# Sliding-window attention into a gated feed-forward: the first v loads, the GpSimd queue and the planned arrival times

## The chip, the core and the metric

The kernel runs on one core of a Trainium2 chip. The metric is the device time of one execution in microseconds (us). "Before" was run nine times; its median is 320.32 us, the fastest run 319.82 and the slowest 321.81. Engines are named PE (matrix products), DVE (VectorE), ACT (ScalarE), POOL (GpSimd) and SP (SyncE). Loads are issued from POOL's instruction queue, in order with POOL's other work, and are carried out by 16 shared DMA engines.

## The reference

Eight batches, eight heads, 576 positions, head width 64. Heads 0 to 3 attend to the last 32 positions ("plain"); heads 4 to 7 attend to 32 positions at a stride of 4 ("dilated"). The result, 4608 rows of 512, goes through two matrix products with a gate between them.

```python
mask_plain = (rel >= 0) & (rel < window)                       # window = 32
mask_dil = (rel >= 0) & (rel < window * dilation) & (rel % dilation == 0)   # dilation = 4
scores = scale * np.matmul(q, k.transpose(0, 1, 3, 2))         # masked, softmax over the last axis
x = (attn @ v).transpose(0, 2, 1, 3).reshape(B * S, H * D)
h = x @ w_in                                                   # 512 -> 2048
g = h * (1.0 / (1.0 + np.exp(-h)))
out = g @ w_out                                                # 2048 -> 512
```

Inputs and output are float32; inside, the kernel works in float16 with float32 sums. The cast of q, k, v and the weights is done by the loads themselves, which POOL issues.

## The kernel before

**Tiles.** Attention runs per batch. For batches 0 to 2 k and q are loaded as rows (`nat`) and turned on PE (steps TD, TA, TR, TS, TB); later batches are turned by DMA. Scores (steps S) are computed in sets, exponentiated on ACT into `probs`, and multiplied with v (steps P for plain heads with tile `vp`, steps D for dilated heads with tile `vd`). DVE divides by the row sums (L659, L660). Steps XP and XD turn the result into x. Layer 1 (L861) makes 16 blocks h per group of rows, ACT makes tanh (L870), DVE makes gT (L872), and layer 2 (L894) needs all 16. The first two groups have 256 rows, the others 512.

**v of the first batch.** `vraw` holds v for the dilated heads in two halves. A copy brings each half into `vd`, whose last column of ones gives the row sums: half 0 by step V 0, on DVE (L481), and half 1 by the entry `c0` of the load list, on POOL (L232). Tile `vp` is filled by two loads, the first of only 96 rows (L178, below 32 rows of zeros written by L183), the second of the other 23 windows (L179).

**Masks.** For the first batch the mask is added to the scores on PE (L595). It comes from a tile `band`, which POOL makes (L194, L196) and DVE turns into `mask_d` and `mask_p` (L202 to L206).

**The order of loads** is written out by hand and issued by POOL after the first loads:

```python
ORDER = "k0 r0 w0a w0b c0 w1 w2 w3 d1 p1 r1 o0 v1 o1 o2 o3".split()
```

Here k0 are the last 48 rows of k and q, r0 is the second half of `vraw`, w0a to w3 are w_in in column blocks of 256 or 512, d1, p1, r1 and v1 are k and q (dilated, then plain), `vraw` and `vp` of batch 1, and o0 to o3 are w_out in four parts.

**The planner.** The order of PE, ACT and DVE instructions is found by a small model at build time (class `Plan`). It gives each step a cost and each load an arrival time: `AT_DIL`, `AT_PLAIN`, `AT_VRAW`, `AT_VP` for the first tiles of a batch, and for the list a running sum that starts at `AT_W0` and grows by `LOAD_US` for each entry. A step is placed no earlier than the arrival that it needs. On the chip nothing waits for a planned time: the times decide only the order in which each engine's instructions stand. `best` chooses between DVE and ACT for copies.

Of the kernel before, what the change touches and what calls it, by code (L numbers as in the profile page):

```python
# [10 lines left out]
F32 = mybir.dt.float32  # L11
# [5 lines left out]
def kernel(  # L17
# [9 lines left out]
    nc = tc.nc  # L27
    B, H, S, D = q.shape
    DM, DFF = moe_w_in.shape
    P = 128  # L30
    W = 32
# [5 lines left out]
    QB = P - W  # L37
# [14 lines left out]
    XR = 3  # L52
    NA = GA * GT
    BIG = 32768.0
    ORDER = "k0 r0 w0a w0b c0 w1 w2 w3 d1 p1 r1 o0 v1 o1 o2 o3".split()
    LOAD_US = {"w": 2.75, "o": 2.6, "d": 3.7, "p": 3.7, "r": 1.4, "v": 2.6, "k0": 2.0, "r0": 1.2, "c0": 0.0, "w0a": 1.4, "w0b": 1.4}
    AT_W0 = 10.6
    BIASED = (0,)

    cpool = ctx.enter_context(tc.tile_pool(name="const", bufs=1))  # L60
# [14 lines left out]
    xRs = [cpool.tile([P, HP, GT], F16, name=f"xR_{i}") for i in range(XR)]  # L75
# [4 lines left out]
    vps = [cpool.tile([P, HN * NB, 66], F16, name=f"vp_{i}") for i in range(NV)]  # L80
    vds = [cpool.tile([P, 2, HN, DIL, 66], F16, name=f"vd_{i}") for i in range(NV)]
    vraws = [cpool.tile([P, 2, HN, DIL, D], F16, name=f"vraw_{i}") for i in range(NV)]
# [23 lines left out]
    def nat_of(b, key):  # L106
        i = ("k", "q", "rest").index(key)
        return nats[b % 2][:MA, i * RW : (i + 1) * RW].rearrange("p (h r d) -> p h r d", h=H, r=DIL)
# [5 lines left out]
    def issue_nat(b, h0, h1):  # L114
        for nm, src, m0 in (("k", k, 0), ("q", q, MR)):
            rows = src[b].rearrange("h (m r) d -> m h (r d)", r=DIL)
            r0 = M - MR if nm == "k" else 0
            p0 = 0 if nm == "k" else MR
            for d, at in ((nat_of(b, nm), m0), (nat_of(b, "rest")[p0 : p0 + MR], r0)):
                nc.gpsimd.dma_start(  # L120
                    out=d[:, h0:h1].rearrange("p h r d -> p h (r d)"),
                    in_=rows[at : at + d.shape[0], h0:h1],
                )

    def issue_part(src, m0, m1, dst, h0, h1):
        rows = src[0].rearrange("h (m r) d -> m h (r d)", r=DIL)
        nc.gpsimd.dma_start(  # L127
            out=dst[: m1 - m0, h0:h1].rearrange("p h r d -> p h (r d)"), in_=rows[m0:m1, h0:h1]
        )

    def issue_first(h0, h1):
        issue_part(k, 0, MA, nat_of(0, "k"), h0, h1)
        issue_part(q, 0, MA, nat_of(0, "q"), h0, h1)
# [22 lines left out]
    def issue_vraw(b, halves=(0, 1)):  # L156
        vraw = vraws[b % NV]
        src = v[b, HN:].rearrange("h (m r) d -> m h (r d)", r=DIL)
        for ab in halves:
            p0, m0, m1 = ((0, 0, VA), (VB - KB, VB, M))[ab]  # L160
            nc.gpsimd.dma_start(  # L161
                out=vraw[p0 : p0 + m1 - m0, ab].rearrange("p h r d -> p h (r d)"),
                in_=src[m0:m1],
            )

    def v_win(t0, n, step=S * D):
        flat = v.rearrange("b h s d -> (b h s) d")
        win = flat[t0 : t0 + P]
        return bass.AP(
            tensor=win.tensor, offset=win.offset, ap=[win.ap[0], [step, n], win.ap[1]]  # L170
        )

    def issue_vp(b):
        nc.gpsimd.dma_start(out=vps[b % NV][:, :, :D], in_=v_win(b * H * S - W, HN * NB, QB * D))  # L174

    def issue_vp_first():
        flat = v.rearrange("b h s d -> (b h s) d")
        nc.gpsimd.dma_start(out=vps[0][W:, 0, :D], in_=flat[:QB])  # L178
        nc.gpsimd.dma_start(out=vps[0][:, 1:, :D], in_=v_win(QB - W, HN * NB - 1, QB * D))  # L179

    for t in vraws[::-1]:
        nc.vector.memset(t, 0.0)
    nc.vector.memset(vps[0][:W, 0, :], 0.0)  # L183
    nc.vector.memset(kqDs[0][:, :, :, 0, MA:], 0.0)
    for t in vps:
        nc.vector.memset(t[:, :, D:], 1.0)
# [1 line left out]
        nc.vector.memset(t[:, :, :, :, D:], 1.0)  # L188
    for t in kPs:
        nc.vector.memset(t[:, :, :W], 0.0)  # L190
    issue_first(HN, H)
    issue_first(0, HN)
    make_identity(nc, ident)
    nc.gpsimd.memset(band, 1.0)  # L194
    for s, base in ((1, 0), (-1, W - 1)):
        nc.gpsimd.affine_select(  # L196
            out=band, in_=band, compare_op=ALU.is_ge, fill=0.0, base=base,
            pattern=[[s, P]], channel_multiplier=-s,
        )
    issue_vraw(0, (0,))  # L200
    issue_vp_first()
    nc.vector.tensor_scalar(band, band, 1.0, BIG, ALU.subtract, ALU.mult)  # L202
    nc.vector.tensor_copy(mask_d[:, :6], band[:, None, :MH].broadcast_to([P, 6, MH]))
    nc.vector.tensor_copy(mask_d[:, 6:], band[:, None, P - MH :].broadcast_to([P, 4, MH]))
# [9 lines left out]
    AT, AT_WIN = {}, {}  # L214
    at = AT_W0
    for what in ORDER:
        kind, n = what[0], int(what[1])
        if kind == "w":
            f0, f1 = {"": (0, 4), "a": (0, 2), "b": (2, 4)}[what[2:]]
            cols = slice((4 * n + f0) * P, (4 * n + f1) * P)  # L220
            nc.gpsimd.dma_start(out=w_in16[:, :, cols], in_=wi[:, :, cols])  # L221
        elif kind == "o":
            nc.gpsimd.dma_start(
                out=w_out16[:, 4 * n : 4 * n + 4], in_=wo[:, 4 * n : 4 * n + 4]
            )
        elif what == "k0":
            issue_part(k, MA, M, nat_of(0, "rest"), 0, H)
            issue_part(q, MA, M, nat_of(0, "rest")[MR:], 0, H)
        elif what == "r0":
            issue_vraw(0, (1,))  # L230
        elif what == "c0":
            nc.gpsimd.tensor_copy(vds[0][:, 1, :, :, :D], vraws[0][:, 1])  # L232
        elif kind == "d":
            issue_nat(n, HN, H)
        elif kind == "p":
            issue_nat(n, 0, HN)
        elif kind == "r":
            issue_vraw(n)
        else:
            issue_vp(n)  # L240
        at += LOAD_US[what] if what in LOAD_US else LOAD_US[kind]
        AT[what] = at
        if kind == "w":
            for f in range(f0, f1):
                AT_WIN[4 * n + f] = at
# [83 lines left out]

    plan = Plan()  # L330
    t2 = at
    AT_DIL = {0: 5.4, 1: AT["d1"], 2: t2 + 7.0}
    AT_PLAIN = {0: 7.5, 1: AT["p1"], 2: t2 + 7.0}
    AT_VRAW = {0: 8.6, 1: AT["r1"], 2: t2 + 8.6}
    AT_VP = {0: 10.6, 1: AT["v1"], 2: t2 + 11.4}
    AT_CAST = t2 + 18.0
    AT_REST = AT["k0"]
    AT_V1 = AT["r0"] + 1.2
    AT_WOUT = [AT[f"o{n}"] for n in range(4)]

    readers = {}
# [94 lines left out]
    def attention(b):  # L436
        pe_path = b < PEB
        at_vraw, at_vp = (AT_VRAW[b], AT_VP[b]) if b < 3 else (v_in[b], v_in[b])
        sets, masks, home = SETS[pe_path], MASKS[pe_path], HOME[pe_path]
# [37 lines left out]
        def copy_on(eng, dst, src):  # L477
            if eng == "ACT":
                nc.scalar.copy(dst, src)  # L479
            else:  # L480
                nc.vector.tensor_copy(dst, src)  # L481

        def best(dve, act):
            ends = {
                e: max(plan.now, plan.free[e]) + us for e, us in (("DVE", dve), ("ACT", act))
            }
            return ("DVE", dve) if ends["DVE"] + LEAN * (b == 0) <= ends["ACT"] else ("ACT", act)
# [139 lines left out]
        def paired(key):  # L627
            step = best(0.335, 0.95)
            yield step
            src = nat_of(b, key)  # L630
            copy_on(
                step[0], pairs[key].rearrange("p g r i d -> p i g r d"),
                src[:, :HP].rearrange("p (g i) r d -> p i g r d", i=2),
            )
# [4 lines left out]
                nc.vector.tensor_scalar(t, t, 1.0 / BIG, 1.0, ALU.mult, ALU.add)  # L639

        def vd_of(ab):
            if b == 0 and ab == 1:
                return
            step = best(0.335, 0.95) if pe_path else ("DVE", 0.335)
            yield step
            copy_on(step[0], vd[:, ab, :, :, :D], vraws[b % NV][:, ab])
# [107 lines left out]
        for key in order:  # L754
# [3 lines left out]
            if kind == "N":  # L758
                st = Step(lambda ring, a=a: paired(*a), 0.0, (), [AT_PLAIN[b]], ("DVE",))
            elif kind == "B":  # L760
# [3 lines left out]
            elif kind == "TA" and b == 0:  # L764
                st = Step(
                    lambda ring, a=a: trans_a0(ring, *a), 0.36, rings,
                    [AT_PLAIN[0]],
                )
            elif kind == "TD" and b == 0:
                st = Step(lambda ring, a=a: trans_d0(ring, *a), 0.17, rings, [AT_DIL[b]])  # L770
            elif kind == "TR":
# [12 lines left out]
            elif kind == "TD":  # L784
                st = Step(lambda ring, a=a: trans_d(ring, *a), 0.28, rings, [AT_DIL[b]], ("DVE",))
            elif kind == "S":
# [15 lines left out]
            elif kind == "V":  # L802
                st = Step(lambda ring, a=a: vd_of(*a), 0.0, (), [AT_V1 if b == 0 and a[0] else at_vraw], ())
            elif kind == "P":
# [135 lines left out]
    while att or l1 or l2:  # L940
# [15 lines left out]
        for q_, it, lim in cands:  # L956
            r = plan.ready(it[1])
            if r is None:
                continue
            r = max(r, plan.t + plan.backlog(it[1].uses) - lim)  # L960
# [42 lines left out]
```

## Time and profile before

| | |
|---|---|
| median of nine runs | 320.32 us (319.82 to 321.81) |
| profiled execution, its own time | 321.78 us |
| span in that profile | 320.0 us |
| PE busy | 303.0 us (95%) |
| DVE busy | 195.0 us (61%) |
| ACT busy | 164.2 us (51%) |
| POOL busy | 54.4 us (17%) |
| moved by DMA | 44.49 MB, mean 139 GB/s |

The profile is one execution; its own time is 1.46 us above the median, and 1.78 us of its time lie outside the span. The chain of waits counts back from the last instruction. Two thirds of the kernel (from about 60 us on) PE is busy without a gap of note; the places where PE stands still are in the first 60 us and in the last 4 us. DMA is busy in all of the first 150 us except for one short stretch.

### The profile page before, as it was taken

What the parts mean: (1) busy time and instruction counts of PE and PEld (TensorE: products, weight loads), DVE (VectorE), ACT (ScalarE), POOL (GpSimd) and SP (SyncE); (2) the same over time, 40 slices, a digit from 0 to 9 for tenths busy, and PEclk for the clock granted to TensorE, in tenths of its full rate; (3) what the DMA queues carried; (4) which work ended last, traced back from release to release, by engine and by line L of the source; (5) the groups of instructions that cost most, each with busy time, mean ns of one, the idle gap of its engine ahead of it and who ended that gap; (6) DMA issues with size and microseconds to landing.
All of it is one profiled execution on the core that took longest, in us unless ns stands there. A gap on an engine that the chain in (4) does not pass through costs nothing.

```text
span 320.0 us, 6092 instructions
## 1 busy us (share of the span) xinstructions
PE 303.0 (95%) x2378; PEld 154.8 (48%) x2378; DVE 195.0 (61%) x493; ACT 164.2 (51%) x300; POOL 54.4 (17%) x87
## 2 busy tenths in 40 slices
PE   2998689999999999999999999999999999999994
PEld 1576575655445444544454444444544444444442
DVE  4348798899779777853885687548741553355000
ACT  7577566566665365453663564545442453355111
POOL 8463833000810032004200410000000000000000
PEclk9999999999999999999999999999999999999999
DMA  7989999999999959998999799962191000100221
GB/s 94 164 107 202 198 191 191 206 213 178 97 198 240 190 113 186 200 209 145 186 235 173 134 195 192 189 163 73 51 179 38 33 35 33 66 33 2 80 84 66
DMA packets 107124, 44.49 MB, mean 139 GB/s; under 512 B 73304, under 2 KB 102488, under 8 KB 107096
## 3 DMA queue, kind: packets, MB, share of 16 engines
q0 software_dynamic: 48960, 19.92, 51.8%
q1 hardware_dynamic: 52952, 14.75, 26.7%
q10 hardware_dynamic: 5184, 9.44, 8.5%
q8 instruction: 18, 0.29, 0.4%
q14 instruction: 10, 0.08, 0.1%
HBM read 39.84 MB, written 18.28 MB: 182 GB/s over the span
## 4 chain that ended last, share of the span: by engine, by line
PE 83%; DMA 8%; POOL 4%; ACT 2%; DVE 1%; issue 1%; ACTq 0%; POOLq 0%
PE y L894 38%; PE h L861 36%; PE s L607 3%; DMA w_in<-in_moe_w_in_dram 3%; DMA vraw<-in_v_dram 3%; DMA w_out<-in_moe_w_out_dram 2%; PE av_p L656 2%; PE av_d L656 2%; POOL nat L127 1%; ACT ob L905 1%; POOL vraw L161 1%; POOL vp L179 0%; POOL w_in L221 0%; DVE gT L872 0%; PE xd L710 0%
## 5 line engine op out<-in xcount | busy, mean ns | idle before, releaser
L894 PE MATMUL y<-w_out,gT 128*128 128x512 f16 x576 | 138.6, 379 | 1.7 <-ACT ob L905 1.1
L872 DVE SCALAR_TENSOR_TENSOR gT<-th,h 128x512 f16<-128x512 f32 (+1 forms) x160 | 98.3, 628 | 59.0 <-ACT th L870 58.8
L870 ACT ACTIVATE th<-h 128x512 f32<-128x512 f32 (+1 forms) x160 | 88.3, 555 | 81.5 <-PE h L861 77.2
L861 PEld LDWEIGHTS <-w_in 128*128 128x128 f16 x640 | 58.3, 98 | 55.4 <-issue 2.6
L894 PEld LDWEIGHTS <-gT 128*128 128x128 f16 x576 | 53.8, 98 | 61.2 <-issue 2.0
L861 PE MATMUL h<-xR,w_in 128*128 128x512 f16 x320 | 77.9, 379 | 0.2 <-DVE gT L872 0.2
L861 PE MATMUL h<-xA,w_in 128*128 128x512 f16 (+1 forms) x320 | 65.6, 339 | 1.9 <-DMA w_in<-in_moe_w_in_dram 1.0
L616 ACT ACTIVATE probs<-s 128x768 f16<-128x768 f32 (+2 forms) x47 | 36.4, 774 | 20.2 <-PE s L607 17.6
L905 ACT ACTIVATE ob<-y 128x512 f32<-128x512 f32 x36 | 21.5, 598 | 39.9 <-PE y L894 39.8
L656 PEld LDWEIGHTS <-probs 128*128 128x128 f16 x448 | 22.7, 100 | 11.6 <-issue 0.4
L660 DVE TENSOR_TENSOR oD<-av_d,rcps 72x256 f16<-72x256 f32 x64 | 26.9, 421 | 2.2
L660 DVE TENSOR_TENSOR oP<-av_p,rcps 96x256 f16<-96x256 f32 x48 | 20.2, 421 | 1.6
L397 POOL COPY fence<-kqT 128x1 f16<-128x1 f16 x10 | 1.8, 188 | 97.3 <-DMA kqT<-kq_s 97.3
L659 DVE RECIPROCAL rcps<-av_p 96x4 f32<-96x4 f32 x48 | 8.4, 174 | 14.4 <-PE av_p L656 14.1
L625 DVE TENSOR_TENSOR probs<-probs,mask_p 128x768 f16<-128x768 f16 x21 | 11.6, 553 | 5.9 <-ACT probs L616 5.9
L656 PE MATMUL av_d<-vd,probs 128*128 128x65 f16 x256 | 14.4, 198 | 0.3 <-ACT qP L479 0.3
L659 DVE RECIPROCAL rcps<-av_d 72x4 f32<-72x4 f32 x64 | 11.0, 172 | 5.9 <-PE av_d L656 5.5
L656 PE MATMUL av_p<-vp,probs 128*128 128x65 f16 x192 | 13.3, 198 | 0.0
L625 DVE TENSOR_TENSOR probs<-probs,mask_d 128x576 f16<-128x576 f16 (+1 forms) x23 | 11.8, 514 | 2.0 <-ACT probs L616 1.8
L161 POOL DMA_DIRECT2D vraw<-in_v_dram x16 | 10.8, 677 | 6.6 <-DVE oD L660 2.2
L174 POOL DMA_DIRECT2D vp<-in_v_dram x7 | 10.1, 1444 | 2.1 <-PE xp L698 1.8
L481 DVE COPY vd<-vraw 128x1024 f16<-128x1024 f16 x14 | 6.3, 453 | 3.5 <-DMA vraw<-in_v_dram 3.5
(86 smaller groups left out, 143.7 us busy)
## 6 DMA issues: line engine op xcount, KB each, us to landing
out_dram<-ob ACTq DMA_DIRECT2D x36, 256.0 KB, 3.0
kq_s<-in_k_dram POOLq DMA_DIRECT2D x5, 576.0 KB, 10.1
kq_s<-in_q_dram POOLq DMA_DIRECT2D x5, 576.0 KB, 12.9
vp<-in_v_dram POOLq DMA_DIRECT2D x7, 384.0 KB, 8.7
w_out<-in_moe_w_out_dram POOLq DMA_DIRECT2D x4, 512.0 KB, 11.5
vraw<-in_v_dram POOLq DMA_DIRECT2D x8, 224.0 KB, 6.0
w_in<-in_moe_w_in_dram POOLq DMA_DIRECT2D x3, 512.0 KB, 7.2
x_s<-oP SPq DMA_DIRECT2D x10, 144.0 KB, 4.0
```

Of the source, the lines that this page charges most:

```text
L161: nc.gpsimd.dma_start(out=vraw[p0 : p0 + m1 - m0, ab].rearrange("p h r d -> p h (r d)"), in_=src[m0:m1],)
L174: nc.gpsimd.dma_start(out=vps[b % NV][:, :, :D], in_=v_win(b * H * S - W, HN * NB, QB * D))
L616: nc.scalar.activation(p2, both[:, :, :n], AF.Exp, scale=scale)
L625: nc.vector.tensor_tensor(p2, p2, mk, ALU.mult)
L656: nc.tensor.matmul(a[:, i, : D + 1], lhs(i), rhs(i), start=True, stop=True)
L659: nc.vector.reciprocal(rcp[:n], a[:n, :, D : D + 1])
L660: nc.vector.tensor_tensor(o, a[:n, :, :D], rcp[:n, :, None].broadcast_to([n, HN, D]), ALU.mult)
L861: nc.tensor.matmul(h[:, :w], w_in16[:, c, f * P : (f + 1) * P], x_g[:, c], start=(c == 0), stop=(c == HP - 1),)
L870: nc.scalar.activation(th[:, :w], h[:, :w], AF.Tanh, scale=0.5)
L872: nc.vector.scalar_tensor_tensor(gTs[g][:, f, :w], th[:, :w], 1.0, h[:, :w], ALU.add, ALU.mult)
L894: nc.tensor.matmul(y, gTs[g][:, f, tb * P : (tb + 1) * P], w_out16[:, f], start=(f == 0), stop=(f == NFF - 1),)
L905: nc.scalar.activation(ob, y, AF.Copy, scale=0.5)
```

## The change

1. The entry `c0` leaves the list. The second half of `vd` for batch 0 is then made like the first, by step V 1 on DVE or ACT, as `best` chooses. POOL has no copy left there.
2. POOL issues the load of the first half of `vraw` ahead of `band`, not behind it.
3. The first 96 rows for `vp` come as float32 by a load from SP into `v_head`, a borrowed piece of a tile that is not yet in use, and DVE casts them into `vp`. The zeros above them are written into `v_head`. This DVE cast stands ahead of the instruction that turns `band` into a mask.
4. Planned arrivals: `AT_W0` 10.6 to 12.6, the four first-tile times later by 0.9 to 2.3 us, `LOAD_US` a little smaller for the weights and r0, `AT_V1` without its 1.2 us for the copy.

```diff
-    ORDER = "k0 r0 w0a w0b c0 w1 w2 w3 d1 p1 r1 o0 v1 o1 o2 o3".split()
-    LOAD_US = {"w": 2.75, "o": 2.6, "d": 3.7, "p": 3.7, "r": 1.4, "v": 2.6, "k0": 2.0, "r0": 1.2, "c0": 0.0, "w0a": 1.4, "w0b": 1.4}
-    AT_W0 = 10.6
+    ORDER = "k0 r0 w0a w0b w1 w2 w3 d1 p1 r1 o0 v1 o1 o2 o3".split()
+    LOAD_US = {"w": 2.6, "o": 2.6, "d": 3.7, "p": 3.7, "r": 1.4, "v": 2.6, "k0": 2.0, "r0": 0.9, "w0a": 1.3, "w0b": 1.3}
+    AT_W0 = 12.6
...
     def issue_vp_first():
-        flat = v.rearrange("b h s d -> (b h s) d")
-        nc.gpsimd.dma_start(out=vps[0][W:, 0, :D], in_=flat[:QB])
         nc.gpsimd.dma_start(out=vps[0][:, 1:, :D], in_=v_win(QB - W, HN * NB - 1, QB * D))
+    v_head = xRs[2][:, 0, : 2 * D].bitcast(F32)
...
-    nc.vector.memset(vps[0][:W, 0, :], 0.0)
+    nc.vector.memset(v_head[:W], 0.0)
...
+    nc.sync.dma_start(out=v_head[W:], in_=v[0, 0, :QB])
     issue_first(HN, H)
     issue_first(0, HN)
     make_identity(nc, ident)
+    issue_vraw(0, (0,))
     nc.gpsimd.memset(band, 1.0)
...
-    issue_vraw(0, (0,))
     issue_vp_first()
+    nc.vector.tensor_copy(vps[0][:, 0, :D], v_head)
     nc.vector.tensor_scalar(band, band, 1.0, BIG, ALU.subtract, ALU.mult)
...
-        elif what == "c0":
-            nc.gpsimd.tensor_copy(vds[0][:, 1, :, :, :D], vraws[0][:, 1])
...
-    AT_DIL = {0: 5.4, 1: AT["d1"], 2: t2 + 7.0}
-    AT_PLAIN = {0: 7.5, 1: AT["p1"], 2: t2 + 7.0}
-    AT_VRAW = {0: 8.6, 1: AT["r1"], 2: t2 + 8.6}
-    AT_VP = {0: 10.6, 1: AT["v1"], 2: t2 + 11.4}
+    AT_DIL = {0: 6.3, 1: AT["d1"], 2: t2 + 7.0}
+    AT_PLAIN = {0: 9.5, 1: AT["p1"], 2: t2 + 7.0}
+    AT_VRAW = {0: 10.4, 1: AT["r1"], 2: t2 + 8.6}
+    AT_VP = {0: 12.9, 1: AT["v1"], 2: t2 + 11.4}
...
-    AT_V1 = AT["r0"] + 1.2
+    AT_V1 = AT["r0"]
...
-            if b == 0 and ab == 1:
-                return
```

## The prediction, made before the changed kernel ran

> **What bounds the kernel now.** I read the page first, for which engine fills the span and where it does not.
>
> ```profile
> span 320.0 us, 6092 instructions
> PE 303.0 (95%) x2378; PEld 154.8 (48%) x2378; DVE 195.0 (61%) x493; ACT 164.2 (51%) x300; POOL 54.4 (17%) x87
> ```
>
> PE is the bound: 320.0 - 303.0 = 17.0 us is all that it stands still. The table by stretches places it: 6.9 us before 10 us (the first loads), 0.2 us from 10 to 26, 5.1 us from 26 to 60, 0.8 us from 60 to 300, and 4.0 us behind the last matmul. Only the first three can be reached by this change. PE's waits name their causes:
>
> ```profile
> PE td L532 <- DMA nat<-in_k_dram: 5.2, 1, 5.2
> PE td L518 <- DMA nat<-in_q_dram: 1.6, 1, 1.6
> ...
> PE h L861 <- DMA w_in<-in_moe_w_in_dram: 1.0, 1, 1.0
> PE ta_k L558 <- DMA nat<-in_k_dram: 1.0, 1, 1.0
> PE h L861 <- DVE gT L872: 1.0, 2, 0.8
> ...
> PE y L894 <- DMA w_out<-in_moe_w_out_dram: 0.5, 1, 0.5
> ```
>
> Three of them, 1.6 + 1.0 + 0.5, are late loads of weights and of batch 1. Why these are late stands in POOL's timeline:
>
> ```profile
> 9.47 0.71 POOL L161 DMA_DIRECT2D vraw<-in_v_dram  x1
> 10.17 1.51 POOL L221 DMA_DIRECT2D w_in<-in_moe_w_in_dram  x2
> 18.71 1.04 POOL L232 COPY vd<-vraw 128x1024 f16<-128x1024 f16 x1 [7.02 <-DMA vraw<-in_v_dram]
> 19.69 2.23 POOL L221 DMA_DIRECT2D w_in<-in_moe_w_in_dram  x3
> ```
>
> POOL is done with w0b at 11.68, then stands 7.02 us before the copy c0 until its data land, copies for 1.04, and only then issues w1 to w3 and all that is behind them. Whether DMA had other work meanwhile is shown by the stretches of 2 us (last two columns: DMA share and GB/s):
>
> ```profile
> 16.00:18.00 2.00, 1.97 (x31) 1.75 (x29) 1.20 (x5) 1.61 (x4) 0.00 (x0) 1.00 1.38 189
> 18.00:20.00 2.00, 2.00 (x30) 1.28 (x30) 0.75 (x3) 1.51 (x5) 1.29 (x2) 1.00 0.23 30
> 20.00:22.00 2.00, 2.00 (x24) 1.14 (x19) 0.60 (x2) 1.60 (x6) 2.00 (x4) 1.00 0.48 19
> 22.00:24.00 2.00, 2.00 (x27) 1.45 (x26) 1.20 (x5) 1.02 (x4) 2.00 (x4) 1.00 1.16 188
> ```
>
> It had not: up to 18 us and from 22 us on DMA moves 188 to 213 GB/s in most stretches, and between them it is nearly empty. So c0 costs DMA time, and PE pays for it later, at 26 to 58 us, where DMA is full and PE waits for it.
>
> **c0 leaves POOL: the main term.** In 18 to 22 us DMA moved 2 x 30 + 2 x 19 = 98 KB; at 190 GB/s it would have moved 760 KB. The missing 660 KB are 3.5 us: the upper end of what every later load can gain. The lower end: w0b, issued at 10.9, takes 9.8 us to land (its row among the DMA issues), so 20.7; w1 lands 5.4 us behind 19.69, at 25.1, of which 512 KB at 200 GB/s are 2.6, so its data began at about 22.5 and cannot begin before 20.7 on the slowest of the 16 engines: 1.8 us. I take 2.8, nearer to the byte count, since most engines were empty already at 18 us. POOL's own issue is no limit: w1 to w3 then go out from about 11.2. Issues do wait, each for the landing of the load eight before it (25.38 behind w1's landing at 25.1, 27.95 behind w2, 31.42 behind w3), but with eight loads in flight DMA has work throughout.
>
> Against PE's waits: w3 lands at 31.2 - 2.8 = 28.4, and PE reaches it at 30.14, so 1.0 us goes. PE is then at the first td of batch 1 at 31.4 instead of 32.5; the last of d1 lands at 34.2 - 2.8 = 31.4, so 1.6 goes: 2.7 in all. The wait for gT at 40 us (0.8) stands behind the pair copies of batch 1 (DVE, 38.0 to 39.3), which come earlier with their loads; half of it goes, 0.4. PE is then at its first y at 41.87 - 0.54 - 2.7 - 0.4 = 38.2, while o0 lands at 41.8 - 2.8 = 39.0. What is late next is therefore o0, by 0.8 us, and the gain there is held to 2.8. The new plan puts o0 at 37.3 instead of 36.25 (sum of the list), so a little more other work stands ahead of it and covers some of this: 3.0 us is my figure for the term. From 60 us on PE has no idle time to give or to lose, so the gain is kept to the end.
>
> **The copy's new place.** V 1 now stands in DVE's queue. The nearest row is the first half's copy on DVE, 0.72 us at 10.46 us (other such copies average 0.45); on ACT the same shape takes 1.04. DVE has this gap:
>
> ```profile
> 18.36 0.41 DVE L481 COPY xA<-xp 128x192 f16<-128x192 f16 x2
> 20.55 0.18 DVE L659 RECIPROCAL rcps<-av_p 96x4 f32<-96x4 f32 x1 [1.78 <-PE av_p L656]
> ```
>
> The half landed at 18.65; the copy ends by 19.4 and costs nothing as long as it ends before 20.55. Without that cover it costs 0.7. Behind it in the queue are the divisions of L659 and L660, for which PE's XP waits.
>
> **The Trainium skill against this.** SBUF — State Buffer, section "SBUF: two separate sides", warns that a DVE copy in a two-port mode keeps GpSimd from writing the descriptors of its loads. The 0.72 against 0.45 is the only trace of a meeting here, and it fell on the copy. By the rule POOL's issues would halt for up to 0.72 us; by the rows DVE pays 0.27. In both cases DMA is by then eight loads deep, so I count zero, with 0.7 as the other end.
>
> **vraw before band, and 96 rows over SP.** POOL saves the issue of L178, 0.55 us, and puts 0.65 us of vraw ahead of the 0.9 us of band. The queue becomes: vraw 4.7 to 5.4, band to 6.3, vp to 7.8 (before 8.2), k0 to 9.0, r0 to 9.7, w0 to 11.25. No PE wait hangs on these, as DMA was backed up already (134 to 193 GB/s from 8 to 16 us), so the gain is zero to 0.4; I take zero. band is done 0.65 us later, at 6.3; the masks then follow for about 1.4 us, until 7.7 (before 6.94), and PE first reads one at 9.04: 1.3 us of cover. On DVE the cast of v_head waits for the SP load, with band's masks queued behind it. Small loads land in 3.0 to 4.4 us in this profile (output stores 3.0, the 12 KB it replaces 4.4). SP's queue holds nothing else; issued at about 1 us it lands by 5.4, before band. Both ends: nothing, or, if it landed at 9 us, about 1.5 us on the first scores. The cast is 64 columns wide, less than the 0.2 of a 192-column copy, in DVE's wait of 1.96 us.
>
> **Later planned times.** They change the order, at no price of their own. First arrivals are now planned near the landings (AT_DIL 6.3, q landed at 6.15; AT_VRAW 10.4, landed at 10.46), so the first scores may come ahead of TA instead of behind its 1.0 us wait: up to 0.3 us gained, since their inputs are ready only at 8.2. What I cannot cost is the clock. The granted clock reads 1.00 throughout, but PE's pace doubles:
>
> ```profile
> 21.28 1.03 PE L861 MATMUL h<-xA,w_in 128*128 128x256 f16 x4
> 22.11 0.37 PE L698 MATMUL xp<-ident,oP 96*128 96x96 f16 x2
> ...
> 23.94 0.61 PE L861 MATMUL h<-xA,w_in 128*128 128x256 f16 x4
> 24.39 0.41 PE L656 MATMUL av_d<-vd,probs 128*128 128x65 f16 x8
> ```
>
> From start to next start four h matmuls take 0.83, later 0.45. TensorE: Matmul & The Clock Gate, section "What's actually happening", says that about 3.4 us of sustained work lift the clock to full. By that rule it would be full from 13 us whatever the order, and the new order would cost nothing. The trace disagrees: PE is busy from 8.6 us and slow until 22.7. So small matmuls seem not to count, and an order that brings layer 1 earlier or later by one such window moves the end by half of 3.4: 1.7 us either way. I put zero in the sum and keep both ends for the range.
>
> **Sum.** Span 320.0 - 3.0 = 317.0. With 1.78 us outside the span that is 318.8 against the profiled execution's 321.78; this stands 1.46 above the median, so in terms of the median 317.3 us.
>
> **Rivals.**
> - *Only the slowest DMA engine counts* (14%). The loads gain little more than 1 us, as w0b's landing at 20.7 suggests. Against it: DMA share is 0.23 at 18 us, few engines at work. 320.3 - 1.2 = 319.1.
> - *All waits go, and the clock rises earlier* (13%). The 5.1 us of idle time from 26 to 60 shrink to about 1.5, and half a window is won: -5.0, 315.3. Against: o0 and DVE, which is busy 30 of the 36 us from 24 to 60.
> - *No gain* (7%): DVE takes the place of DMA. 30.2 us of its work plus V 1 in 33 us instead of 36 leave 2 us of slack; a bad order turns all of the gain into waits for gT. 320.3.
> - *Slower: V 1 blocks DVE* (11%). DVE works in order, and V 1 is planned from 15.5 while its half landed at 18.65. A landing later than 20.55 - 0.72 = 19.8 pushes all divisions back, us for us, and beats the 3.0 gained from 22.8 on. At 24 us it would give 321.5. Against it: the load is issued 0.4 earlier with the same loads ahead. For it: on POOL a late half blocked loads only, on DVE it blocks PE.
>
> **How the numbers follow.** The main case has 55%, with its own range 316.2 to 318.6. About 0.3% (1 us) can be told from no change. Faster: 55 + 14 + 13 = 82%; within it 7%; slower 11%. The range takes in the second and most of the third and fourth case: 315.2 to 319.9.
>
> **What would show it.** POOL without its 7.02 us wait, w1 to w3 issued at 11 to 14 us; no stretch below 150 GB/s from 18 to 22 us; w3 landing near 28.4; PE waiting for no w_in at 31 us, for nat at most 0.3 us, and possibly for w_out. V 1 on DVE near 19 us with no long wait before it. It is wrong if loads land less than 1.5 us earlier, if DVE waits for vraw past 20 us, or if PE's idle time from 26 to 60 us stays near 5 us with DVE or ACT as the releaser.

## The result and the profile after

After runs in 318.70 us (median of 18 runs, 317.43 to 321.59) against 320.37 for before (55 runs). The ratio is 0.9946, 95% interval 0.993 to 0.9961: 1.7 us faster, between 1.2 and 2.2. The forecast was 317.3, 3.0 us faster: the direction was right and the time lies in the stated range, but the gain is little more than half of the forecast. The execution of after that is read below took 319.92 us, 1.2 above its median, as that of before was 1.46 above its own.

The page of after, its span and the busy times:

```profile
span 318.2 us, 6091 instructions
PE 303.0 (95%) x2378; PEld 155.0 (49%) x2378; DVE 196.0 (62%) x489; ACT 165.4 (52%) x306; POOL 53.1 (17%) x85
```

PE is busy for as long as in before, 303.0 us; it stands still 15.2 us instead of 17.0. POOL's timeline of after (start, duration, instruction, in brackets the idle time before it and what ended it):

```profile
8.97 0.71 POOL L161 DMA_DIRECT2D vraw<-in_v_dram  x1
9.68 2.99 POOL L222 DMA_DIRECT2D w_in<-in_moe_w_in_dram  x4
14.37 0.75 POOL L222 DMA_DIRECT2D w_in<-in_moe_w_in_dram  x1 [1.71 <-DMA vp<-in_v_dram]
15.11 0.69 POOL L120 DMA_DIRECT2D nat<-in_k_dram  x1
```

w1 and w2 follow w0 at once; w3 waits for the landing of the load eight before it, and the first load of batch 1 is issued at 15.11 instead of 21.89. The stretches of 2 us (last two columns DMA share and GB/s) show that the gap is closed:

```profile
18.00:20.00 2.00, 2.00 (x34) 1.29 (x31) 1.02 (x4) 1.26 (x5) 0.85 (x2) 1.00 1.26 207
20.00:22.00 2.00, 2.00 (x25) 1.19 (x22) 0.93 (x3) 1.76 (x6) 0.39 (x1) 1.00 1.24 207
```

PE's waits in after (total us, times, longest):

```profile
PE td L531 <- DMA nat<-in_k_dram: 5.2, 1, 5.2
PE xp L695 <- DVE oP L657: 1.7, 3, 0.9
PE y L891 <- ACT ob L902: 0.9, 2, 0.4
PE ta L492 <- DVE gT L869: 0.8, 2, 0.6
PE td L531 <- DMA nat<-in_q_dram: 0.7, 1, 0.7
PE td L542 <- DMA nat<-in_q_dram: 0.6, 1, 0.6
PE av_d L653 <- ACT kP L478: 0.4, 1, 0.4
PE av_p L653 <- DVE probs L624: 0.3, 1, 0.3
PE s L594 <- DVE mask_d L204: 0.3, 1, 0.3
PE av_d L653 <- DVE probs L624: 0.2, 1, 0.2
```

All waits for w_in, w_out and batch 1 (3.1 us) are gone. In their place stand DVE and ACT, and a wait for k0 (L542) that the profile of before did not have. By stretch, PE's idle time goes from 6.9 to 6.2 us before 10 us, from 0.2 up to 1.4 between 10 and 26, from 5.2 to 3.3 between 26 and 60, from 0.8 to 0.3 up to 300, and is unchanged (3.97 and 3.92) behind the last matmul. The sum is the span's 1.8 us.

### The profile page after: what moved, and what is told of

Same layout as the page of the kernel before. It is cut to its first block, busy times and chain, and to the rows that moved or that the text cites. A ratio compares the mean times of both kernels' runs of the same rounds, so it can differ in the third digit from the quotient of the medians.

```text
span 318.2 us, 6091 instructions
## 1 busy us (share of the span) xinstructions
PE 303.0 (95%) x2378; PEld 155.0 (49%) x2378; DVE 196.0 (62%) x489; ACT 165.4 (52%) x306; POOL 53.1 (17%) x85
## 4 chain that ended last, share of the span: by engine, by line
PE 84%; DVE 8%; DMA 2%; POOL 2%; ACT 2%; issue 1%; ACTq 0%; DVEq 0%; POOLq 0%
PE y L891 38%; PE h L858 36%; PE s L606 3%; DVE gT L869 3%; DMA nat<-in_q_dram 2%; PE av_d L653 2%; PE av_p L653 2%; POOL nat L127 1%; DVE oP L657 1%; DVE probs L624 1%; DVE vd L480 1%; DVE oD L657 1%; ACT ob L902 1%; PE xp L695 1%; DVE rcps L656 1%
## 5 line engine op out<-in xcount | busy, mean ns | idle before, releaser
L858 PEld LDWEIGHTS <-w_in 128*128 128x128 f16 x640 | 59.0, 98 | 53.6 <-issue 1.0
L858 PE MATMUL h<-xA,w_in 128*128 128x512 f16 (+1 forms) x320 | 64.8, 340 | 0.1
L902 ACT ACTIVATE ob<-y 128x512 f32<-128x512 f32 x36 | 21.5, 597 | 44.2 <-PE y L891 43.7
L653 PE MATMUL av_p<-vp,probs 128*128 128x65 f16 x192 | 12.6, 198 | 0.3 <-DVE probs L624 0.3
L480 DVE COPY vd<-vraw 128x1024 f16<-128x1024 f16 x16 | 8.5, 535 | 2.2 <-DMA vraw<-in_v_dram 2.2
## 6 DMA issues: line engine op xcount, KB each, us to landing
w_out<-in_moe_w_out_dram POOLq DMA_DIRECT2D x4, 512.0 KB, 12.6
```

The costliest lines, as they stand in the source:

```text
L653: nc.tensor.matmul(a[:, i, : D + 1], lhs(i), rhs(i), start=True, stop=True)
L858: nc.tensor.matmul(h[:, :w], w_in16[:, c, f * P : (f + 1) * P], x_g[:, c], start=(c == 0), stop=(c == HP - 1),)
L902: nc.scalar.activation(ob, y, AF.Copy, scale=0.5)
```

## The experiments

All were timed against before on the same chip, except the last, which is a single execution.

**The parts of the change.** e1 takes c0 alone out of before; e2 gives before the planned times alone (`LOAD_US` with them); e3 is after with the old times; e8 is c0 and the times together, without the moves of vraw and of the 96 rows.

e1_c0_only:
```diff
-    ORDER = "k0 r0 w0a w0b c0 w1 ...
+    ORDER = "k0 r0 w0a w0b w1 ...
-    AT_V1 = AT["r0"] + 1.2
+    AT_V1 = AT["r0"]
-            if b == 0 and ab == 1:
-                return
```


> Before, with one edit: the copy c0 leaves POOL and becomes step V 1 (planned from the arrival of r0); band, vraw, the first 96 rows and all other planned times stay as before. Theory 'load gap': the whole gain of the change comes from closing the DMA gap, so POOL has no 7 us wait, no stretch from 18 to 22 us is below 150 GB/s, the third block of w_in lands near 27 us, PE waits for no w_in, and the time is 318.0 to 319.2. Rival 'times': the later planned times carry the gain; without them the new arrivals meet an unfit order and the time stays at 319.7 to 320.7.

Measured: 320.22 us, in the range of the rival; ratio 0.9981 (0.9963 to 0.9999), 0.6 us. DMA is full as expected (197 and 208 GB/s at 18 to 22 us), and w3 lands at 15.23 + 13.2 = 28.4. But PE, with the old order, still waits 3.4 us for loads, no less than before:

```profile
PE td L518 <- DMA nat<-in_q_dram: 1.8, 1, 1.8
PE y L892 <- DMA w_out<-in_moe_w_out_dram: 1.2, 1, 1.2
...
PE h L859 <- DMA w_in<-in_moe_w_in_dram: 0.4, 1, 0.4
```

Closing the gap alone is worth 0.6 us, between 0.0 and 1.2: "the whole gain of the change comes from closing the DMA gap" missed.

e2_times_only:
```diff
-    AT_W0 = 10.6
+    AT_W0 = 12.6
-    AT_DIL = {0: 5.4, ...    AT_PLAIN = {0: 7.5, ...
+    AT_DIL = {0: 6.3, ...    AT_PLAIN = {0: 9.5, ...
-    AT_VRAW = {0: 8.6, ...   AT_VP = {0: 10.6, ...
+    AT_VRAW = {0: 10.4, ...  AT_VP = {0: 12.9, ...
```


> Before, with only the planned times of the change (AT_W0, the four first-tile times, LOAD_US); the copy c0 stays on POOL, so the DMA gap stays. Theory 'load gap': loads land as before, PE still waits for w_in and batch 1 from 26 to 60 us, and the time is 319.9 to 321.0. Rival 'times': 318.5 to 319.3 without any change of the loads.

Measured: 319.70, ratio 0.9973 (0.9959 to 0.9988), 0.9 us, between the ranges of the two theories. The times alone gain. The gap stays (50 GB/s from 18 to 20 us), and yet PE waits for no w_in, and for batch 1 only this:

```profile
PE td L518 <- DMA nat<-in_q_dram: 0.6, 1, 0.6
```

e3_old_times:
```diff
-    AT_W0 = 12.6      (and LOAD_US and the four first-tile times, in after)
+    AT_W0 = 10.6
```


> After, with the planned times of before (the copy on DVE or ACT, vraw ahead of band and the 96 rows over SP stay). Theory 'load gap': the loads land as in after; the order of before has TR behind other work, so the wait for k0 near 16 us (0.55) should be gone, and the time is 317.5 to 318.8, equal to after or up to 1 us better. Rival 'times': 319.5 to 320.5.

Measured: 319.08, ratio 0.9951 (0.993 to 0.9972), 1.6 us: with the loads of the change the planned times hardly matter. The gain is about that of after, as the first theory had it (its range ended at 318.8), but the waits are others: that for k0 shrank to 0.2, and waits of 1.6 for batch 1 and 0.8 for w_out came back.

e8_times_and_c0 (e1 and e2 together):
```diff
-    ORDER = "k0 r0 w0a w0b c0 w1 ...     AT_W0 = 10.6
+    ORDER = "k0 r0 w0a w0b w1 ...        AT_W0 = 12.6
```


> Before, with the copy c0 gone from POOL and all the planned times of the change; band stays ahead of vraw and the first 96 rows stay on POOL. It completes the square of the parts: c0 alone gave 0.6 us, the times alone 0.9, all but the times 1.6, all together 1.7. Theory 'two halves': c0 and the times together carry nearly all, 1.2 to 1.7 us (318.8 to 319.3), and the moves of vraw and the 96 rows are worth no more than 0.4. Rival 'the moves': these, one load less for the limit of eight in flight and 0.5 us earlier issues, carry about 1 us, and the time is 319.4 to 320.0.

Measured: 318.96, ratio 0.9961 (0.9936 to 0.9986), 1.2 us, at the theory's lower end. By the ratios c0 is worth 0.6, the times 0.9, both 1.2, all but the times 1.6, all 1.7; each figure has an interval of 0.5 to 0.8 us either way, so whether the parts add up cannot be told. The moves of vraw and the 96 rows make the difference between e1 and e3 (1.0 us) and between e8 and after (0.5); these intervals overlap, and no run has the moves alone. The landings further down say more of them.

PE's waits for w_in, batch 1 and w_out go by another line than c0. With the old times they are 3.1 us in before (4.2 in e12 below), 3.4 in e1 and 2.4 in e3; with the new ones 0.6 in e2, 0.8 in e4 and nothing in e8 and after. But the pace divides nearly the same traces. The first four h matmuls take 0.44 us from start to next start in e1, e3 and e12, and 0.69 to 0.83 in e2, e4, e8 and after, where PE thus comes later to all loads behind them; and e5, with all new times but one and again 0.44, waits 3.2 us. Whether the order or the pace takes these waits away is not settled.

**The copy itself.** e4 puts c0 back on POOL, behind w3.

```diff
-    ORDER = "... w1 w2 w3 d1 ...
+    ORDER = "... w1 w2 w3 c0 d1 ...      # c0: nc.gpsimd.tensor_copy, as in before
```


> After, but with the copy of the second half on POOL, behind w3 in the list. Theory 'load gap': it is the wait of POOL ahead of w1 that cost, not the copy; behind w3 the half has landed, POOL waits for nothing, DMA stays full, and the time is within 0.5 us of after (318.2 to 319.2); DVE is relieved of 0.41 us. Rival 'the copy itself': moving 1 us of work off DVE, which is busy 29 of 34 us from 26 to 60, gives another 0.5 to 1 us; or, if any POOL work between the loads costs, the time goes back towards 320.

Measured: 318.88, ratio 0.9944 (0.9923 to 0.9965), the same as after. POOL still waits for the half there, which the first theory did not expect:

```profile
17.20 1.04 POOL L233 COPY vd<-vraw 128x1024 f16<-128x1024 f16 x1 [1.79 <-DMA vraw<-in_v_dram]
```

With w1 to w3 issued ahead of it DMA has work meanwhile (206 GB/s from 18 to 20 us). So c0 behind w3 is as good as c0 gone; that DVE now makes the copy is worth nothing measurable.

**The order.** e5 repairs the wait for k0.

```diff
-    AT_REST = AT["k0"]
+    AT_REST = AT["k0"] + 1.6
```


> After, with one planned time moved: AT_REST (k0, the last rows of k and q) 1.6 us later, 16.2 instead of 14.6; in after its q half landed at 15.9 and PE stood 0.55 us for it with P 0 and P 1 queued behind. The order then has P 0, P 1 ahead of TR and layer 1 a little earlier. Theory 'early order': the change gave back 1.2 us of PE idle time between 10 and 26 us, of which this repairs 0.5 to 1.0: 317.7 to 318.3. Rival 'cover': PE's early waits are hidden by DVE, which is the next bound from 26 to 60 us; the time stays within 0.3 us of after (318.7).

Measured: 320.28, ratio 0.9976 (0.9956 to 0.9995). A miss of both: the wait is gone, layer 1 starts at 18.6 instead of 21.5, and the gain over before is smaller than that of after (the intervals just meet). Its PE waits:

```profile
PE ta L492 <- DVE gT L869: 1.5, 1, 1.5
PE td L517 <- DMA nat<-in_q_dram: 1.2, 1, 1.2
PE h L858 <- DMA w_in<-in_moe_w_in_dram: 1.0, 1, 1.0
PE y L891 <- DMA w_out<-in_moe_w_out_dram: 1.0, 1, 1.0
```

PE comes earlier to loads that land no earlier (w3 at 28.3, in after at 27.1). And after these stops the granted clock (third column from the end) falls:

```profile
38.00:40.00 2.00, 1.00 (x15) 0.82 (x12) 1.88 (x7) 1.49 (x5) 0.23 (x1) 0.93 2.17 169
40.00:42.00 2.00, 2.00 (x12) 0.90 (x11) 0.36 (x2) 0.00 (x0) 0.63 (x1) 0.50 1.62 188
42.00:44.00 2.00, 2.00 (x29) 1.54 (x27) 1.47 (x6) 1.18 (x2) 0.65 (x1) 0.71 1.24 206
```

That is about 3.4 us at half clock, or by my estimate 1.7 us of work. Its times fall in two groups, five of 317.8 to 319.1 and seven of 320.3 to 321.0; the mean clock on record is 0.998 to 1.000 in the first and 0.989 to 1.000 in the second. That such a fall separates them is argued, not shown.

**PE's half pace.** e6 (on after) and e7 (on before) put seven extra matmuls ahead of PE's first transpose, e9 (on after), e10 (on e3) and e11 (on before) eleven. The extra work is on a zeroed tile.

```diff
+    for n in range(7):                       # e6, e7: on the zeroed vraws[1], 2.1 to 5.2 us
+        nc.tensor.matmul(warm, flat0[:, :P], flat0[:, :GT], start=True, stop=True)
...
+    nc.vector.memset(xA[:, 0, :GT], 0.0)     # e9 to e11: nine on this tile from 1.3 us,
+    warm_up(9)                               # and warm_up(2) behind the first transpose
```

> After, with seven extra matmuls of 512 columns on a zeroed tile ahead of PE's first transpose (from about 2 to 5 us, when PE has nothing to do); they add work and change no result. Theory 'clock': PE's half pace up to 22 to 25 us waits for dense matmuls; with them it is at full pace much earlier, the first h comes at 19 to 20 us instead of 21.5, and the time falls by 1 to 2 us against after, to 316.7 to 317.7. Rival 'window': three microseconds are too short or the sparse transposes behind them let the pace fall back; the pace changes at the same place as in after and the time stays at 318.7 plus or minus 0.4, or rises by up to 0.3 where the extra matmuls run past 5.2 us.

> Before, with the same seven extra matmuls. Theory 'clock': PE reaches its late loads earlier and waits longer for them, since the loads set the pace from 26 to 60 us there; the time falls by less than in after, 0 to 0.7 us, to 319.7 to 320.5, so that the change is worth 2.5 to 3.5 us once the pace is out of the way. Rival 'window': 320.2 to 320.9, and the change is worth the same as without.

> After, with nine extra matmuls from about 1.4 us (on a tile that is zeroed first) and two more behind PE's first transpose, where PE waits for q: 4.9 us of dense work instead of 3.2. In the run with seven of them the pace rose at 14.5 us, fell at 17.9 and rose again at 21.3, steps of 3.4 us. Theory 'clock': with more of a step filled the pace is full from 8 to 11 us in most executions and the time is 316.0 to 317.5. Rival 'enough': after is bound by k0 and DVE once the pace is early, and the time stays at 317.5 to 318.2 as with seven; the two in the wait for q may cost up to 0.2 us.

> The loads of the change with the planned times of before (319.1 us without extra matmuls), plus the same eleven extra matmuls. Theory 'order': the old order leads PE into the loads (nat, w_out) once the pace is early, as in before, so this gains less than after does: 317.8 to 319.0. Rival 'loads only': the planned times don't matter once the loads are early, and it is within 0.4 us of the same extra matmuls on after.

> Before, with the same eleven extra matmuls. With seven it was unchanged (320.6), PE waiting 2.4 us for w_in instead of 1.0. Theory 'loads bind': still 319.9 to 320.9, however early the pace rises. Rival 'clock alone': a pace that is full from 8 us shows in before too, 318.5 to 319.5.

| | ratio to before (95%) | median us |
|---|---|---|
| e6, after + 7 | 0.9921 (0.9892 to 0.995) | 317.89 |
| e7, before + 7 | 0.9999 (0.9983 to 1.0015) | 320.58 |
| e9, after + 11 | 0.9923 (0.9898 to 0.9949) | 318.31 |
| e10, e3 + 11 | 0.994 (0.9918 to 0.9962) | 318.51 |
| e11, before + 11 | 1.0032 (1.0011 to 1.0053) | 321.83 |

Before gains nothing from the extra work; with eleven it even loses 1 us, outside what was expected. Seven did not show an effect on the pace: in e7 the fifteen transposes behind them take 1.38 us, as in before, and the first four h matmuls 0.45. That is earlier than in the profile of before that was read (0.83), but the same as in e12 below (0.44), which has no extra work, and so is PE's wait for w_in. First e7, then e12:

```profile
PE h L865 <- DMA w_in<-in_moe_w_in_dram: 2.4, 3, 1.2
```
```profile
PE h L861 <- DMA w_in<-in_moe_w_in_dram: 2.4, 3, 1.4
```

Eleven did: in e11 the fifteen transposes take 0.89 us. There PE waits 6.4 us for these loads, which agrees with "loads bind":

```profile
PE td L526 <- DMA nat<-in_q_dram: 2.1, 2, 1.6
PE td L553 <- DMA nat<-in_q_dram: 1.6, 1, 1.6
PE y L904 <- DMA w_out<-in_moe_w_out_dram: 1.5, 1, 1.5
...
PE h L871 <- DMA w_in<-in_moe_w_in_dram: 1.2, 2, 0.7
```

On after the extra work brings 0.8 us by the ratios, twice, with six runs each, but each interval overlaps that of after; e6 is the fastest version run, clearly faster than before and not clearly faster than after. Its 317.89 lies between the ranges of its two theories, and the first four h matmuls in it still take 0.83. A full pace from early on did not come about in e9 either: the fifteen transposes took 0.81 us instead of 1.38, but from 12 to 22 us the granted clock was near 0.5 again. e9's 318.31 lies just above both of its ranges, and e10's 318.51 fits both of its own, so they tell nothing apart.

**The profile that was read.** In e2, e7 and e11, whose loads up to c0 are those of before, POOL waited only 5.3 to 5.6 us at c0. So before was profiled once more.

> Before, unchanged, profiled once more. In three kernels whose loads up to c0 are those of before (the times alone, and the two with extra matmuls) POOL waited 5.3 to 5.6 us at c0, not 7.0. Theory 'late half': the execution that the prediction read had an unusually late second half of vraw; here the wait is 5.2 to 5.8, the half lands near 17.1, and DMA misses 300 to 420 KB of its rate between 18 and 22 us instead of 660. Rival 'other kernels': the shorter wait belongs to those kernels' other edits, and the wait is 6.7 to 7.2 again.

Measured: 320.01 us, PE busy 300.0 us instead of 303.0, and a wait at c0 of 4.98 us, just under the range of the first theory. POOL's line and the two stretches:

```profile
16.66 1.04 POOL L232 COPY vd<-vraw 128x1024 f16<-128x1024 f16 x1 [4.98 <-DMA vraw<-in_v_dram]
```
```profile
18.00:20.00 2.00, 1.83 (x38) 1.35 (x31) 0.70 (x3) 2.00 (x9) 2.00 (x4) 1.00 0.50 40
20.00:22.00 2.00, 2.00 (x30) 1.45 (x28) 1.90 (x8) 1.59 (x5) 2.00 (x4) 1.00 1.20 197
```

The half lands at 16.6, not 18.65; DMA is empty for one stretch, not for two, and misses 2 x (190 - 40) = 300 KB, not 660. In four of five executions with these loads the wait is 5.0 to 5.6. The prediction had read the fifth.

## Why the prediction came out as it did

**On the side of the loads the mechanism held.** c0 held up w1 to w3 and DMA ran empty for it; with c0 gone, or behind w3, it does not. V 1 runs on DVE at 21.15 without a wait before it; the slower rival did not happen. On the side of PE it is only in part shown. In the profile of after the three waits have vanished and o0 binds no longer, but from 26 to 60 us only 1.9 us of idle time went, since DVE and ACT stand in the place of the loads; and e1, which has c0's going and little else, keeps such waits.

**The mis-sized term is the advance that the loads gain from c0, "I take 2.8".** Here is when loads land, from issue and time to landing, in every profile of this case. c0 is in its old place in five (before, e12, e2, e7, e11); it is gone and nothing moved in two; seven have the moves of vraw and the 96 rows as well (after, e3, e5, e6, e9, e10, and e4 with c0 behind w3).

| us | before, as read | c0 in place, median of five | c0 gone: e1, e8 | with the moves, median of seven |
|---|---|---|---|---|
| w3 | 31.1 | 29.6 | 28.4, 28.6 | 27.5 |
| last of d1 | 34.2 | 32.6 | 31.6, 32.0 | 30.8 |
| o0 | 41.8 | 40.2 | 40.2, 39.5 | 38.9 |
| o3 | 52.0 | 50.4 | 50.4, 51.5 | 49.2 |

The going of c0 brings w3 forward by 1.1 us, o0 by 0.4 and o3 not at all, and in time, alone, 0.6 us (e1). The execution that was read had a late half and landed its loads about 1.6 us later than the median of the five, and the working carried its gap over in full. The lower bound of 1.8 us was the better figure, and "little more than 1 us", the rival of the slowest DMA engine, came nearest. That the late half also made that execution slow is not shown: it is 1.7 us longer in span than e12, but PE is busy 3.0 us longer in it and idle 1.3 us less.

**"So the gain is zero to 0.4; I take zero"**, for vraw and the 96 rows, failed. Where they are moved, w3 lands another 1.0 us earlier and o0 0.9, and the time falls by another 0.5 to 1.0 us, though with overlapping intervals. Which of the two does it, and how, stays open. With this and the 0.9 us of the planned times, terms put at nothing gave back part of what the main term lacked: that the total came out at more than half of the forecast is in part luck.

**"From 60 us on PE has no idle time to give or to lose, so the gain is kept"** held: 0.8 to 0.3 us, and the same tail.

**"They change the order, at no price of their own"** failed both ways. The times alone gain 0.9 us (e2), and in after they put TR, which waits 0.55 us for k0, ahead of P 0; from 10 to 26 us it has 1.2 us more of idle time than before. "Up to 0.3 us" for the first scores was right in kind: they start at 7.84 instead of 9.04.

**The clock**, put at zero with 1.7 either way, was rightly left open. In the same kernel, before, four h matmuls ran at 0.83 us when it was read, and in e12 at 0.44 from 19.04 to 19.48:

```profile
19.04 0.61 PE L861 MATMUL h<-xA,w_in 128*128 128x256 f16 x4 [0.17 <-DMA w_in<-in_moe_w_in_dram]
19.48 0.25 PE L698 MATMUL xp<-ident,oP 96*128 96x96 f16 x2
```

So the place where the pace rises belongs to the execution, not to the order alone. "Small matmuls seem not to count" does not hold: in e12 the pace had risen ahead of all h matmuls, near the 13 us that the prediction worked out and then took back. The same eight score matmuls, in before and in e12:

```profile
13.84 0.50 PE L607 MATMUL s<-qP,kP 64*128 64x96 f16 x8
```
```profile
13.11 0.34 PE L607 MATMUL s<-qP,kP 64*128 64x96 f16 x8
```

What an early pace is worth in either kernel is not settled: no run sets it.

**The rule on DVE copies and GpSimd** got its trace. DVE's copies in after:

```profile
6.55 1.25 DVE L204 COPY mask_d<-band 128x432 f16<-128x432 f16 x1
...
10.69 0.74 DVE L480 COPY vd<-vraw 128x1024 f16<-128x1024 f16 x1 [2.23 <-DMA vraw<-in_v_dram]
...
21.15 0.41 DVE L480 COPY vd<-vraw 128x1024 f16<-128x1024 f16 x1
```

The vd copy takes 0.74 us while POOL issues loads and 0.41 while POOL is idle, and mask_d takes 1.25 beside the issue of vp (6.23 to 7.72), which costs PE 0.3 us at its first scores. Not every meeting costs: in before the same mask_d copy (5.86 to 6.27) took 0.41 beside the issue of vraw (5.55 to 6.20). SBUF — State Buffer, section "Who interferes with whom", says that whichever starts first holds the port and the other is blocked; here it was DVE that waited, and POOL's issue of vp was no longer for it (1.49 us, in before 1.50). The prediction's cover of 1.3 us for the masks was used up, as the first scores came 1.2 us earlier.

## What to carry to other kernels

Before a wait in the queue that issues loads is given a price, look at the bytes moved in that stretch; here it was as good to put the waiting instruction behind the issues as to take it away (e4). Before a wait's length is made into a gain, read it in more than one execution: here it was 7.0 us in one and 5.0 to 5.6 in four. A term put at zero deserves a run of its own: the planned times and the moves brought no less than the main term, as far as the intervals tell. And two profiles of the same kernel can differ in pace (PE busy 303.0 and 300.0 us), so PE's waits in two kernels are compared where the pace is alike.

## What was not expected of the hardware

PE fell back to half clock after a standstill and stayed there although it was busy: in e8, PE stood 2.7 us for k0's q, and the granted clock (third column from the end) was down for ten us.

```profile
14.00:16.00 2.00, 0.14 (x5) 0.01 (x1) 0.00 (x0) 0.59 (x2) 0.75 (x1) 0.92 1.46 201
16.00:18.00 2.00, 1.19 (x16) 1.10 (x16) 0.11 (x1) 0.33 (x1) 1.26 (x2) 0.50 1.43 192
...
22.00:24.00 2.00, 2.00 (x25) 1.57 (x25) 0.59 (x4) 1.56 (x5) 0.58 (x1) 0.50 1.25 207
24.00:26.00 2.00, 2.00 (x16) 0.99 (x15) 1.61 (x5) 0.43 (x2) 0.19 (x1) 0.52 1.27 203
26.00:28.00 2.00, 1.96 (x33) 1.72 (x32) 1.32 (x5) 1.80 (x4) 0.48 (x1) 1.00 1.42 195
```

From 20 to 26 us PE is busy all the time, with matmuls of 65 to 384 columns, at half clock: here being busy did not raise it for nearly 6 us. And ahead of the first change the column can read 1.00 where the pace is half, as in before at 21.28 us, so the pace from start to start is the safer reading.
